# First feed-forward product of the last 1024 tokens as seven half-size products, with PSUM tiles and SBUF taken over from attention

## The chip, the cores and the metric

The kernel runs on one core of one Trainium2 chip. The metric is the device time of one execution in microseconds (us). The engines are called by their short names: PE (TensorE; its weight loads are listed apart as PEld), DVE (VectorE), ACT (ScalarE), POOL (GpSimd) and SP (the queue that issues most transfers). PSUM is the memory that PE writes its sums to, SBUF the memory that all engines work in.

## What is computed

Attention for 8 batches of 8 heads, 576 tokens each, head size 64, with a threshold, and then a feed-forward layer over all 4608 tokens. All of it is fp32.

```python
scores = scale * np.matmul(q, k.transpose(0, 1, 3, 2))
thresh = np.max(scores, axis=-1, keepdims=True) - tau
scores = np.where(scores >= thresh, scores, -1000000000.0)
...
x = np.ascontiguousarray(attn_out.transpose(0, 2, 1, 3)).reshape(B * S, H * D)
h = x @ w_in                                # (4608, 512) @ (512, 2048)
g = h * (1.0 / (1.0 + np.exp(-1.702 * h)))
return (g @ w_out)                          # (4608, 2048) @ (2048, 512)
```

## The kernel before

**Attention** goes by pairs of heads, `n` from 0 to 31, four pairs to a batch. For a pair, PE makes scores by tiles of 128 keys and a last one of 64 (L376, L383), ACT copies them out of PSUM (`keep`, L406), DVE takes their greatest value in several steps (`in_groups` L420, `over_tiles` L426 and L431, `over_groups` L438 and L439), subtracts it (`sub`, L490 and L495), ACT masks and takes exponentials (L501, L505), PE multiplies by the values (`values`, L519), and DVE makes the sums of the exponentials (again L420 to L439), turns and inverts them (`one_group` L558, `spread_sums` L567 and L569) and writes the scaled result to the tiles `xT` (`place_x`, L586).

**The feed-forward layer** goes by blocks of 256 tokens, 0 to 17. For blocks 2 to 17, `feed_forward` first makes the hidden values: eight panels `j`, each of two times 128 of the 2048 hidden columns. A panel is eight matmuls of 128x128 by 128x256 (`mm1`, L601, each of them two PE instructions), one tanh on ACT (L610) and one combination on DVE (L613). The second product is then done in the Winograd form of Strassen's method: seven products of half size instead of eight (`product`, L691). The sums of its left operands are made on POOL (`s_sums` L669 to L671, `s_last` L676), the seven products are joined by DVE (`read`, L713; the first by ACT, L706), and two stores follow.

**The order of work** is written out by a planner. Each step is a `task` with an engine, a cost, a rank and the tasks that it follows; `run_in_order` plays them through with these costs and issues the instructions in the order that comes out. Each engine then executes its own list strictly in this order, and waits on semaphores. Feed-forward matmuls have the last rank on PE, so they fill what attention leaves, and four blocks are left when attention ends. The first tokens of block 14 are done when batch 6 is, those of blocks 15 to 17 when pair 31, the last, is placed.

**PSUM** is eight banks: `psA` has three tiles of two banks (scores, products with values), `psM` two tiles of one bank (all of the feed-forward layer). **SBUF** for attention comes from a pool `work`: score tiles `s_m` and `s_t`, raw and turned q and k, `mb`, `mbt`, `rc` and `v_m`.

Of the kernel before, what the change touches and what calls it, by code (L numbers as in the profile page):

```python
# [30 lines left out]
def kernel(  # L31
# [75 lines left out]
        for x in range(2)  # L107
# [16 lines left out]

    tasks = []
    NXT = 5
    limits = {"psA": 3, "psM": 2, "s_m": 8, "s_t": 2, "io": 2, "osb": 2, "xT": NXT, "mb": 1,
              "raw0": 1, "raw1": 1, "qkT0": 1, "qkT1": 1, "v_m": 2, "w64": 2, "mbt": 1, "row": 1, "kd": 1, "rc": 1, "v_t0": 1, "v_t1": 1}
    for x in ("raw0", "raw1", "qkT0", "qkT1", "mb"):
        limits[x + "_apart"] = 1  # L130
# [94 lines left out]
    offset = {"raw0": 0, "raw1": S, "qkT0": 2 * S, "qkT1": 3 * S, "mb": 4 * S}  # L225
    offset.update({f"s_m{t}": (6 + 2 * t) * S for t in range(NKT)})

    def home(n, tag, size, name, bufs, key=None):
        if n in APART:
            o = offset[key or tag]  # L230
            return spare[:, o : o + size]
        return work.tile([P, size], FP32, name=name, tag=tag, bufs=bufs)

    def own(n, *pools):
        return tuple(x + "_apart" for x in pools) if n in APART else pools
# [3 lines left out]

    def load_qk(n, which, queue):  # L240
        b, hp = divmod(n, NPAIR)
        name, src = (("q", q), ("k", k))[which]
        t = home(n, f"raw{which}", S, f"{name}_raw", 1)
        blocks = t.rearrange("p (c d) -> p c d", d=32)
        for h in range(2):
            for j in range(2):
                queue.dma_start(  # L247
                    out=blocks[ds(64 * h + 32 * j, 32), :, :],
                    in_=src[b, 2 * hp + h, :, ts(j, 32)].rearrange("(c p) d -> p c d", p=32),
                )  # L250
        raws[n, which] = t

    def load_v(n):
        b, hp = divmod(n, NPAIR)
        t = work.tile([P, NKT, 2, D], FP32, name="v_m", tag="v_m", bufs=2)
        for h in range(2):
            nc.sync.dma_start(
                out=t[:, :, h, :],
                in_=v[b, 2 * hp + h, 0:MAIN, :].rearrange("(c p) d -> p c d", p=P),
            )  # L260
            nc.sync.dma_start(
                out=v_t[n % 2][ts(h, D), h, :], in_=v[b, 2 * hp + h, MAIN:S, :]
            )
        vs[n] = t
# [90 lines left out]

    def prep(n, which):

        dst = home(n, f"qkT{which}", S, "qkT", 1)
        nc.vector.transpose(out=dst, in_=raws.pop((n, which)))  # L359
        mats[n, which] = dst  # L360

# [31 lines left out]

    def keep(n, t, c):
        if t == NKT:
            st = work.tile([P, S], FP32, name="s_t", tag="s_t", bufs=2)
            o = halves(st)
        else:
            if c == 0:
                st = home(n, "s_m", 2 * S, "s_m", 8, f"s_m{t}")  # L400
                st = st.rearrange("p (h s) -> p h s", h=2)
            else:
                st = sT[n, t]
            o = st[:, :, ts(c, SH)]
        sT[n, t] = st
        nc.scalar.copy(out=o, in_=pss.pop((n, t, c))[:, :, 0:SH])  # L406
# [15 lines left out]
    def over_tiles(n, op):  # L422

        pm, pt = stats[n, op]
        r = work.tile([P, 2 * QB], FP32, name="red", tag="red", bufs=2)
        nc.vector.tensor_reduce(  # L426
            out=r, in_=pm.rearrange("p t c -> p c t"), axis=AXL.X, op=op
        )
        for h in range(2):
            part = r[ts(h, D), ts(h, QB)]  # L430
            nc.vector.tensor_tensor(out=part, in0=part, in1=pt[ts(h, D), :], op=op)  # L431
        stats[n, op] = r

    def over_groups(n, op):
        r = stats[n, op]
# [24 lines left out]
        nc.vector.transpose(out=o, in_=f)  # L460

    def spread_max(n):
        mb = home(n, "mb", 2 * S, "mb", 1)
        nc.vector.transpose(
            out=mb, in_=stats[n, ALU.max].unsqueeze(2).to_broadcast([P, 2 * QB, 32])
        )
        mbs[n] = mb.rearrange("p (h s) -> p h s", h=2)
# [7 lines left out]
        )  # L475

    def row_in(n):
        mb = home(n, "mb", 2 * S, "mb", 1)
        mbt = work.tile([P, S], FP32, name="mbt", tag="mbt", bufs=1)
        row = rows.pop(n)  # L480
        nc.sync.dma_start(out=mb, in_=row.to_broadcast([P, 2 * S]))
        for h in range(2):
            nc.sync.dma_start(out=mbt[ts(h, D)], in_=row[:, ts(h, S)].to_broadcast([D, S]))
        mbs[n] = mb.rearrange("p (h s) -> p h s", h=2)
        mbts[n] = mbt
# [38 lines left out]
    def values(n, tiles):  # L524
        if 0 in tiles:
            pvs[n] = psA.tile([P, 2, 512], FP32, name="pv", tag="ps")
        v_m, pv = vs[n], pvs[n]
        by_values(
            n, lambda t, h: v_m[:, t, h, :], lambda h: v_t[n % 2][:, h, :],
            [pv[:, c, :] for c in range(2)], tiles,  # L530
        )

    def sums_by_pe(n, tiles, apart):
        if 0 not in tiles:
            ps = pss[n]
        elif apart:
            ps = [psM.tile([P, BANK], FP32, name="den", tag="mo") for _ in range(2)]
        else:
            d = psA.tile([P, 2, 512], FP32, name="den", tag="ps")
            ps = [d[:, c, :] for c in range(2)]  # L540
        pss[n] = ps
        by_values(n, lambda t, h: ones, lambda h: ones_t[:, h, :], ps, tiles)

    def one_row(n):

# [18 lines left out]
    def spread_sums(n):  # L564

        r = rcs[n]
        nc.vector.reciprocal(out=r, in_=r)  # L567
        rc = work.tile([P, S], FP32, name="rc", tag="rc", bufs=1)
        nc.vector.transpose(out=rc, in_=r.unsqueeze(2).to_broadcast([P, QB, 32]))  # L569
        rcs[n] = rc  # L570

# [77 lines left out]
            op0=ALU.add, op1=ALU.mult,  # L649
        )  # L650

    qa = [[g[:, f, :, ts(h, HT)] for f in range(2)] for h in range(2)]
    qb = [[w_out[:, ts(f, HF), ts(m, HM)] for m in range(2)] for f in range(2)]
    s1, s2 = sg
    s3, s4 = qa[1][0], s2
    t1, t2, t4 = tw
    t3 = qb[0][1]

# [6 lines left out]

    def s_sums(k):

        a11, a21, a22, u1, u2 = (y[:, ts(k, 2), :] for y in (qa[0][0], qa[1][0], qa[1][1], s1, s2))
        nc.gpsimd.tensor_tensor(out=u1, in0=a21, in1=a22, op=ALU.add)  # L669
        nc.gpsimd.tensor_tensor(out=u2, in0=u1, in1=a11, op=ALU.subtract)  # L670
        nc.gpsimd.tensor_tensor(out=a21, in0=a11, in1=a21, op=ALU.subtract)  # L671

    def s_last(k):

        a12, u = (y[:, ts(k, 4), :] for y in (qa[0][1], s2))
        nc.gpsimd.tensor_tensor(out=u, in0=a12, in1=u, op=ALU.subtract)  # L676


    P1, P2, P6, P7, P4, P5, P3 = range(7)
    PRODUCTS = [  # L680
        (qa[0][0], qb[0][0], 0, 0), (qa[0][1], qb[1][0], 1, 0), (s2, t2, 0, 1), (s3, t3, 1, 1),
        (qa[1][1], t4, 0, 0), (s1, t1, 1, 0), (s4, qb[1][1], 0, 1),
    ]
    banks = {}

    def product(x, js):
        left, right, k, o = PRODUCTS[x]
        if x == k and js[0] == 0:
            banks[k] = psM.tile([P, BANK], FP32, name="ops", tag="mo")
        for j in range(*js):  # L690
            nc.tensor.matmul(  # L691
                banks[k][:, ts(o, HM)], lhsT=left[:, j, :], rhs=right[:, j, :],
                start=(j == 0), stop=(j == HF - 1),
            )

    def read(x):


        if x == P1:
# [1 line left out]
                osbs[i] = work.tile([P, d_model], FP32, name="osb", tag=f"osb{i}", bufs=1)  # L701
        (c11, c12), (c21, c22) = ([osbs[i][:, ts(m, HM)] for m in range(2)] for i in range(2))
        k, h = PRODUCTS[x][2:]
        ps = banks[k][:, ts(h, HM)]
        if x == P1:
            nc.scalar.activation(out=c21, in_=ps, func=AF.Copy, scale=0.5)  # L706
            return
# [116 lines left out]
    def feed_forward(blk):  # L824
# [3 lines left out]
        for j in range(HF):  # L828
# [11 lines left out]
            )  # L840
            if j % 2:
                sums.append(task("POOL", 2.5, FIRST, s_sums, j // 2, after=[gelus[j - 1], gelus[j]]))
        reads = [None] * 7

        order = [(P1, 0), (P1, 2), (P1, 3)]
        order += [(x, p) for x in range(P2, 7) for p in range(2)]
        for x, p in order:
            js = ((0, 4), (4, 8), (4, 7), (7, 8))[p]
            after = ffn[-1:] + t_ready
            if x in (P1, P2, P4):  # L850
                after += [gelus[j] for j in range(*js)]
            elif x == P3:
                after.append(lasts[p])
            else:
                after += sums[2 * p : 2 * p + 2]

            after += [reads[y] for y in range(x) if PRODUCTS[y][2:] == PRODUCTS[x][2:]]
            ffn.append(task(
                "PE", FFU / 4 * (js[1] - js[0]), LAST, product, x, js, after=after,
                take=("psM",) if x in (P1, P2) and p == 0 else (),  # L860
            ))
            last_mm2[p % 2] = ffn[-1]
            if p in (0, 2):
                continue
            if x == P6:
                lasts = [task("POOL", 1.6, FIRST, s_last, k, after=ffn[-1:]) for k in range(2)]
            if x == P1:
                a = task("ACT", 0.35, FIRST, read, x, after=ffn[-1:], take=("osb", "osb"))
            else:
                a = task(  # L870
                    "DVE", 0.84 if x == P5 else 0.42, FIRST, read, x, after=ffn[-1:] + reads,
                    give=("psM",) if x >= P5 else (),
                )
            reads[x] = a
        for i, x in ((1, P5), (0, P3)):
            task("SP", 0.6, FIRST, store, blk, i, after=[reads[x]], give=("osb",), lag=2.2)

    gelus = {}
    next_blk = 0
# [3 lines left out]
    for n in range(NP):  # L883
# [107 lines left out]
            "DVE", 1.1, r, place_x, n, after=[a, pv], take=("xT",) * len(new), give=("psA", "rc")  # L991
        )
        while hp == NPAIR - 1 and (next_blk + 1) * BLK <= (b + 1) * S:
            if next_blk >= PLAIN:
                feed_forward(next_blk)
            elif next_blk == PLAIN - 1:
                first_blocks()
            next_blk += 1
# [31 lines left out]
```

## Time and profile before

| what | us |
|---|---|
| median of 4 runs (1391.75 to 1392.04) | 1391.87 |
| the profiled execution | 1391.97 |
| its span, from the first instruction to the last | 1390.0 |
| PE busy in the span | 1344.5 |
| DVE busy | 1053.9 |
| ACT busy | 634.2 |
| POOL busy | 295.8 |

The span is shorter than the execution by 1.97 us, which lie before the first and after the last instruction. The profile lists instructions by engine and by the line of the kernel that issued them. Its views used here are the groups by line (count, busy time, mean duration in ns, and the idle time of the engine ahead of them), the chain of waits that ended last (in order of time), the timeline (start, duration, engine, line, and in brackets the idle time just before and what ended it) and busy time by windows with the clock that was granted to PE (1.00 is full). A matmul's end is modelled, and consecutive matmuls overlap: what one adds is read from the distance of the starts.

### The profile page before, as it was taken

The page shows a single profiled execution, that of the slowest core. Times are in us where ns is not written, and L with a number is a line of the kernel's source. Part 1 is how long each engine was busy: PE and PEld are TensorE (multiplying, and loading weights), DVE is VectorE, ACT ScalarE, POOL GpSimd, SP SyncE. Part 2 cuts the span into 40 slices and gives each one's busy share as a digit, 9 for nine tenths or more (in the row PEclk, how much of TensorE's full clock was granted, in tenths as well). Part 3 has the DMA queues.
Part 4 walks back from the last instruction along what each step waited for, and adds up shares of the span by engine and source line. Part 5 has one row for each costly group of instructions (what it writes and reads, how often), then busy time and mean ns, then how long its engine had stood idle before and what let it go on. Part 6 is the DMA issues. An engine that isn't in the chain of part 4 may idle for free.

```text
span 1390.0 us, 18051 instructions
## 1 busy us (share of the span) xinstructions
PE 1344.5 (97%) x6856; PEld 1016.3 (73%) x6856; DVE 1053.9 (76%) x1776; ACT 634.2 (46%) x806; POOL 295.8 (21%) x374
## 2 busy tenths in 40 slices
PE   5778999899999999999999999999999999999999
PEld 3446764477777777777777777777777778888887
DVE  7989999978888888889888888888888887111111
ACT  5964663555454545454545455444545453100100
POOL 1122212212121213122212122131213121211211
PEclk9889999999999999999999999999999999999999
DMA  8784972211111111111111011111110100000000
GB/s 174 201 241 134 304 239 67 68 23 20 41 27 41 27 41 25 35 26 34 29 35 29 18 42 26 42 26 42 26 42 18 42 0 16 1 16 16 1 16 16
DMA packets 205377, 78.70 MB, mean 57 GB/s; under 512 B 192747, under 2 KB 192747, under 8 KB 205291
## 3 DMA queue, kind: packets, MB, share of 16 engines
q1 hardware_dynamic: 195723, 43.71, 15.0%
q0 software_dynamic: 7200, 33.55, 7.1%
q8 instruction: 54, 0.88, 0.3%
q10 hardware_dynamic: 2368, 0.30, 0.2%
q14 instruction: 32, 0.26, 0.1%
HBM read 68.05 MB, written 9.47 MB: 56 GB/s over the span
## 4 chain that ended last, share of the span: by engine, by line
PE 85%; DVE 10%; DMA 2%; issue 1%; SPq 1%; ACT 0%; POOL 0%; ACTq 0%; DVEq 0%; POOLq 0%
PE hps L601 32%; PE ops L691 28%; PE pv L519 9%; PE ps L383 9%; PE hps L641 4%; DVE part L420 2%; PE ps L376 2%; DVE s_m L490 1%; DMA k_raw<-in_k_dram 1%; DMA arena<-in_moe_w_out_dram 1%; SPq L247 1%; DVE arena L340 1%; DVE red L439 1%; DVE w_in L348 0%; PE den L519 0%
## 5 line engine op out<-in xcount | busy, mean ns | idle before, releaser
L601 PE MATMUL hps<-xT,w_in 128*128 128x256 f32 x2048 | 457.5, 381 | 0.0
L601 PEld LDWEIGHTS hps<-xT,w_in 128*128 128x128 f32 x2048 | 385.2, 190 | 69.5 <-issue 18.5
L420 DVE TRANSPOSE_TENSOR_REDUCE part<-s_m 128x36 f32<-128x1152 f32 x228 | 304.7, 1355 | 71.2 <-ACT s_m L406 70.5
L406 ACT COPY s_m<-ps 128x576 f32<-128x576 f32 x240 | 141.2, 641 | 264.0 <-PE ps L383 262.6
L691 PE MATMUL ops<-w_out,arena 128*128 128x256 f32 x1024 | 234.1, 382 | 0.0
L610 ACT ACTIVATE th<-hps 128x512 f32<-128x512 f32 x144 | 85.5, 593 | 292.4 <-PE hps L601 271.6
L691 PEld LDWEIGHTS ops<-w_out,arena 128*128 128x128 f32 x1024 | 192.3, 190 | 36.1 <-issue 10.4
L669 POOL TENSOR_TENSOR arena<-arena 128x256 f32<-128x256 f32 x64 | 51.9, 811 | 611.0 <-DVE arena L613 611.0
L490 DVE TENSOR_TENSOR s_m<-s_m,mb 128x1152 f32<-128x1152 f32 x120 | 180.4, 1540 | 0.8
L691 PE MATMUL ops<-arena 128*128 128x256 f32 x768 | 171.0, 379 | 0.0
L383 PE MATMUL ps<-qkT 64*128 64x288 f32 x960 | 150.6, 435 | 18.1 <-DVE qkT L359 8.4
L501 ACT ACTIVATE s_m<-s_m 128x1152 f32<-128x1152 f32 x120 | 137.3, 1156 | 66.3 <-DVE s_m L490 66.2
L613 DVE SCALAR_TENSOR_TENSOR arena<-th,hps 128x512 f32<-128x512 f32 x128 | 85.8, 670 | 100.9 <-ACT th L610 100.9
L691 PEld LDWEIGHTS ops<-arena 128*128 128x128 f32 x768 | 145.9, 190 | 19.8
L505 ACT ACTIVATE s_m<-s_m,shift,scl 128x1152 f32<-128x1152 f32 x120 | 158.4, 1339 | 1.4
L383 PEld LDWEIGHTS ps<-qkT 64*128 64x128 f32 x960 | 83.8, 189 | 76.5 <-issue 46.4
L519 PE MATMUL pv<-s_m,v_m 128*64 128x288 f32 x960 | 126.0, 414 | 2.1 <-issue 2.1
L713 DVE SCALAR_TENSOR_TENSOR osb<-ops,osb 128x256 f32<-128x256 f32 x112 | 44.5, 408 | 86.0 <-PE ops L691 85.7
L519 PEld LDWEIGHTS pv<-s_m,v_m 128*64 128x64 f32 x960 | 67.1, 138 | 56.3 <-issue 14.8
L676 POOL TENSOR_TENSOR arena<-arena 128x512 f32<-128x512 f32 x32 | 62.6, 1963 | 111.3 <-PE ops L691 111.2
L623 PE MATMUL ops<-w_out,arena 128*128 128x512 f32 x128 | 60.0, 621 | 2.4 <-DVE w_out L348 2.4
L671 POOL TENSOR_TENSOR arena<-arena 128x256 f32<-128x256 f32 x64 | 60.0, 937 | 0.0
(97 smaller groups left out, 1072.9 us busy)
## 6 DMA issues: line engine op xcount, KB each, us to landing
out_dram<-osb SPq DMA_DIRECT2D x36, 256.0 KB, 2.0
q_raw<-in_q_dram SPq DMA_DIRECT2D x120, 72.0 KB, 2.3
k_raw<-in_k_dram SPq DMA_DIRECT2D x116, 72.0 KB, 2.3
v_m<-in_v_dram SPq DMA_DIRECT2D x64, 128.0 KB, 2.4
w_out<-in_moe_w_in_dram POOLq DMA_DIRECT2D x12, 512.0 KB, 5.6
arena<-in_moe_w_out_dram POOLq DMA_DIRECT2D x12, 512.0 KB, 6.1
w_out<-in_moe_w_in_dram POOLq DMA_DIRECT2D x12, 511.6 KB, 7.3
arena<-in_moe_w_out_dram POOLq DMA_DIRECT2D x12, 511.6 KB, 6.9
```

The costliest lines, as they stand in the source:

```text
L383: nc.tensor.matmul(ps[:, h, 0:SH], lhsT=kT[ts(h, D), ts(t, P)], rhs=qT[ts(h, D), ts(c, SH)], start=True, stop=True,)
L406: nc.scalar.copy(out=o, in_=pss.pop((n, t, c))[:, :, 0:SH])
L420: nc.vector.tensor_reduce(out=o, in_=i, axis=AXL.X, op=op, apply_transpose=True)
L490: nc.vector.tensor_tensor(out=s, in0=s, in1=mb, op=ALU.subtract)
L501: nc.scalar.activation(out=s, in_=s, func=AF.Prelu, alpha=STEEP)
L505: nc.scalar.activation(out=s, in_=s, func=AF.Exp, scale=scl, bias=shift)
L519: nc.tensor.matmul(o[c][ts(h, D), 0:SH], lhsT=lhsT, rhs=rhs, start=(t == 0), stop=(t == NKT),)
L601: nc.tensor.matmul(hidden[j][:, ts(f, BLK)], lhsT=w_in[:, c, ds((f * HF + j) * P, P)], rhs=xTs[blk][:, c, :], start=(c == 0), stop=(c == N ...
L610: nc.scalar.activation(out=ths[j], in_=hidden[j], func=AF.Tanh, scale=GELU_SCALE / 2)
L613: nc.vector.scalar_tensor_tensor(out=g[:, :, j, :], in0=two(ths.pop(j)), scalar=1.0, in1=two(hidden.pop(j)), op0=ALU.add, op1=ALU.mult,)
L676: nc.gpsimd.tensor_tensor(out=u, in0=a12, in1=u, op=ALU.subtract)
L691: nc.tensor.matmul(banks[k][:, ts(o, HM)], lhsT=left[:, j, :], rhs=right[:, j, :], start=(j == 0), stop=(j == HF - 1),)
```

## The change

Blocks 14 to 17 no longer go through `feed_forward` one by one, but through `two_blocks` by twos. The first product of 512 tokens is then a product of a 2x2 matrix of quarters (hidden halves by input halves) with another (input halves by blocks), and it is done by seven half-size products too. For each panel these are seven products of two matmuls (`product1`), in place of sixteen matmuls. Each product has a PSUM tile of its own, taken in turn from `psA` and `psM`, five in all. ACT copies the first product to SBUF, DVE adds the other six on (seven additions a panel, `read1`), and tanh and `gelu1` now read from SBUF, once for each of the two blocks. The sums of quarters of `w_in` are made once (four of 128x512 on DVE for the first two panels, twelve on POOL for the rest), those of `xT` four times 128x512 on DVE for each two blocks. The second block's hidden values are held in SBUF, and its sums for the second product (`s_sum1`) are done on DVE. The new SBUF tiles lie in `arena2`, which replaces the pool's attention tiles: these become fixed places in it, with the same number of buffers, handed on in order. The second product is as before, in `psM` for the first of two blocks, in `psA` for the second.

```diff
+    room, end = {}, 0
+    for tag, size, bufs in (
+        ("s_m", 2 * S, 8), ("s_t", S, 2), ("raw0", S, 1), ("raw1", S, 1), ("qkT0", S, 1),
+        ("qkT1", S, 1), ("mb", 2 * S, 1), ("mbt", S, 1), ("rc", S, 1), ("v_m", NKT * 2 * D, 2),
+    ):
+        room[tag] = [(end + x * size, size) for x in range(bufs)]
+        end += bufs * size
+    arena2 = const.tile([P, end], FP32, name="arena2")
...
+    W_SUMS = [
+        (wc[0], wq[1][0], wq[1][1], ALU.add), (wc[1], wc[0], wq[0][0], ALU.subtract),
+        (wc[2], wq[0][0], wq[1][0], ALU.subtract), (wc[3], wq[0][1], wc[1], ALU.subtract),
+    ]
+    def w_sum(x, k, engine):
+        o, a, b = (y[:, :, ts(k, 2 * P)] for y in W_SUMS[x][:3])
+        engine.tensor_tensor(out=o, in0=a, in1=b, op=W_SUMS[x][3])
...
+    def x_sum(blk, x):
+        b11, b12, b21, b22 = (x_quarter(blk, d, h) for d in range(2) for h in range(2))
+        u1, u2, u4 = xsum
+        o, a, b = ((u1, b12, b11), (u2, b22, u1), (b12, b22, b12), (u4, b21, u2))[x]
+        nc.vector.tensor_tensor(out=o, in0=a, in1=b, op=ALU.subtract)
+    BANK_OF = ("psA", "psM", "psA", "psM", "psA")
+    def product1(blk, j, x):
+        b11, b12, b21, b22 = (x_quarter(blk, d, h) for d in range(2) for h in range(2))
+        left, right = (
+            (wq[0][0], b11), (wq[0][1], b21), (wc[1], xsum[1]), (wc[2], b12),
+            (wq[1][1], xsum[2]), (wc[0], xsum[0]), (wc[3], b22),
+        )[x]
...
+        for c in range(2):
+            nc.tensor.matmul(
+                places[j, x], lhsT=left[:, c, ts(j, P)], rhs=right[:, c, :],
+                start=(c == 0), stop=(c == 1),
+            )
+    def read1(j, x):
...
+        for o, a in sums[x]:
+            nc.vector.tensor_tensor(out=o, in0=ps, in1=a, op=ALU.add)
...
+    def s_sum1(x):
+        (a11, _), (a21, a22) = qas[1]
+        o, a, b = ((s1, a21, a22), (s2, s1, a11), (a21, a11, a21))[x]
+        nc.vector.tensor_tensor(out=o, in0=a, in1=b, op=ALU.subtract if x else ALU.add)
...
+    def two_blocks(blk):
+        b = -(-(blk + 1) * BLK // S) - 1
+        xs = [placed[n] for n in range(NP)]
+        first, xd = not done_w, []
+        for x in range(4):
+            if first:
+                done_w.append([task("DVE", 0.66, LAST - 1.0, w_sum, x, 0, nc.vector, after=done_w[-1:][0] if done_w else xs)])
+            after = (xd[-1:] or xs) + (done_w[x][:1] if first else []) + last_product1
+            xd.append(task("DVE", 0.66, LAST - 1.0, x_sum, blk, x, after=after))
+        if first:
+            for k in range(1, HF // 2):
+                for x in range(4):
+                    after = xs + done_w[x - 1][-1:] + done_w[x][-1:]
+                    done_w[x].append(
+                        task("POOL", 1.5, FIRST, w_sum, x, k, nc.gpsimd, after=after)
+                    )
...
         while hp == NPAIR - 1 and (next_blk + 1) * BLK <= (b + 1) * S:
-            if next_blk >= PLAIN:
+            if next_blk >= TAIL:
+                if (next_blk - TAIL) % 2:
+                    two_blocks(next_blk - 1)
+            elif next_blk >= PLAIN:
                 feed_forward(next_blk)
```

## The prediction

> **What bounds the kernel now.** I read the page first, then the chain of waits from 1150 us on, then the timeline there. The page has PE busy for 97% of the span:
>
> ```profile
> PE 1344.5 (97%) x6856; PEld 1016.3 (73%) x6856; DVE 1053.9 (76%) x1776; ACT 634.2 (46%) x806; POOL 295.8 (21%) x374
> ```
>
> The chain of waits over the end of the run (start, duration, engine, tile, line, count) is PE alone, without a gap, up to the last read:
>
> ```profile
> 1175.76 3.65 PE ops L691 x16
> 1179.41 27.63 PE hps L601 x128
> 1207.03 24.17 PE ops L691 x112
> ...
> 1334.81 27.63 PE hps L601 x128
> 1362.43 24.19 PE ops L691 x112
> ```
>
> So blocks 14 to 17 lie behind attention (the last product with values ends at 1175.8) and are bound by PE: 27.63/128 = 0.216 us an instruction. What PE saves there is saved in full, and what makes PE wait there is paid in full. DVE is busy for 8 of each 50 us then, and has room.
>
> **What it removes.** The built program has 3396 matmuls for 3428, 32 fewer, two instructions each: 64 x 0.216 = **13.8 us** less on PE, in four blocks. Up to PE's 2949th matmul (the end of block 13) all five engines' lists stand in the same order as before, with the same waits, but for some loads that wait for one matmul less. The new places of attention's tiles therefore cost nothing, and block 14, which began at 1179.4 after pair 31 was placed (L586, ended 1176.8), loses no early start.
>
> **Panels in their steady state.** A panel is 28 instructions, 28 x 0.216 = 6.05 us of PE. Its DVE work is seven additions at 0.42 (L713 and L586 take 0.42 for 128x256 out of PSUM) and two `gelu1` at 0.69 (L613): 4.3 us. ACT has a copy at 0.38 (L706) and two tanh at 0.60: 1.6 us. The longest loop: the last product of a panel ends, its read 0.42, first `gelu1` 0.69, second tanh done by then or 0.1 later, second `gelu1` 0.69, and only then the next panel's reads, 1.9 us on, when its second product (at 1.73) has just ended. A PSUM tile comes round after five products, 3.5 us after its product ended; the latest read takes 0.6 of that. PE waits for none of it, with 2 us to spare. A wait before every two matmuls: the nearest row is the third product of before (L691, second to fourth piece), which waits for POOL every two matmuls and still has 3.62 us for 16 instructions like the rest, so I take 0. The other end is the row of scores (L383), with 18.1 us idle before 240 groups, 0.075 each; 112 products would lose 8.4 us. The second block's three sums of 128x1024 on DVE (about 1.25 us from L490's 1.35 for 1152) have 3.5 us and more until PE wants them, as one product of the second round takes 16 x 0.216 = 3.46 us: 0.
>
> **The start of the first two blocks.** Here PE must wait, since nothing is left to fill it. Products 1 and 2 need no sums: 1.73 us, till 1181.0. Product 3 needs two sums of weights and two of tokens. All four stand on DVE's list behind pair 31's placing and behind the last read of block 13, which ends at 1179.87:
>
> ```profile
> 1172.96 0.19 DVE L439 TENSOR_TENSOR red<-red,fold 64x36 f32<-64x36 f32 x1
> ...
> 1173.61 0.71 DVE L558 TENSOR_SCALAR r<-red 32x18 f32<-32x18 f32 x4
> ...
> 1175.81 0.95 DVE L586 TENSOR_TENSOR xT<-pv,rc 128x64 f32<-128x64 f32 x4 [0.37 <-PE pv L519]
> 1179.45 0.42 DVE L713 SCALAR_TENSOR_TENSOR osb<-ops,osb 128x256 f32<-128x256 f32 x1 [2.69 <-PE ops L691]
> ```
>
> A sum of 128x512 from SBUF is bounded by L490 (1.35 for 1152 with POOL at rest) and L492 (0.757 for 576), which differ by 1.03 ns an element: 0.69, of which 0.08 overlap the next; I take 0.65. Between them stands the read of product 2 (0.42). If nothing else happens, product 3 begins at 1179.9 + 4 x 0.65 + the wait for product 2 (0.5) + 0.42 = 1183.5, 2.5 to 3.0 us late; product 4 waits 0.4 more for its pair of sums, product 5 1.4 more for one sum, one read, one sum. That is 4.5 us.
>
> **But POOL is in the way.** Its twelve sums of weights, 128x512 each, follow its last old instruction directly. Their real waits are short: the first two only for exponentials that ended by 1134, the others for products with values of pair 31, from 1171.9 on, since their places are pair 31's score tiles. So two run from 1163.5, and ten from 1171.9 to about 1185 without a pause (1.27 us each, L676 in the quiet end). What POOL then does to DVE this trace shows, at 268 us (four POOL sums of 128x1024 in a row; start, duration):
>
> ```profile
> 268.05 0.18 DVE L438 COPY fold<-red 64x36 f32<-64x36 f32 x1
> 268.26 2.24 DVE L439 TENSOR_TENSOR red<-red,fold 64x36 f32<-64x36 f32 x1
> 270.53 2.27 DVE L438 COPY fold<-red 32x36 f32<-32x36 f32 x1
> 272.83 2.28 DVE L439 TENSOR_TENSOR red<-red,fold 32x36 f32<-32x36 f32 x1
> 275.14 2.79 DVE L558 TENSOR_SCALAR r<-red 32x18 f32<-32x18 f32 x4
> ```
>
> ```profile
> 268.06 4.71 POOL L664 TENSOR_TENSOR arena<-w_out,arena 128x1024 f32<-128x1024 f32 x2
> 272.72 4.64 POOL L664 TENSOR_TENSOR w_out<-w_out 128x1024 f32<-128x1024 f32 x2
> ```
>
> Each of DVE's small steps (0.17 to 0.19 alone) lasts until the POOL instruction in flight has ended, and POOL's next one slips in before DVE's next. L420, L569 and L586 are not held. Pair 31 has just this chain: two L431, two each of L438 and L439, four L558, ten steps that took 2.0 us from 1172.36. The first two POOL sums hold L495 at 1164.1, so it starts some 0.5 late, at 1172.9. One step waits for the third sum; two more slip through while the fourth waits for its values (1173.6); seven are left, each behind one sum: from 1175.0 seven ends at 1.25 apart, the last at 1182.5. Then L567 to L586, 2.4 us as before: placed at 1184.9. Read 0.42, first sum, read of product 2, three more sums, less overlaps: 1188.3. Product 3 starts near 1188.4 instead of 1181.1: **7.3 us** idle, then 0.4 and 1.4 as above, and 0.1 at 1167 where a product of block 13 waits for the delayed reads: **9.2 us**. If only one of the four L558 is held, it is 3.75 us less; if every step is held in full and adds its own 0.17, 1 us more.
>
> **The clock after the gap.** A PE gap costs more than itself (idle time before in brackets):
>
> ```profile
> 213.85 5.97 PE L623 MATMUL ops<-w_out,arena 128*128 128x512 f32 x10 [2.38 <-DVE w_out L348]
> ...
> 231.25 20.76 PE L623 MATMUL ops<-w_out,arena 128*128 128x512 f32 x48
> ...
> 280.25 2.29 PE L383 MATMUL ps<-qkT 64*128 64x288 f32 x8 [6.37 <-DVE xT L586]
> 282.47 3.22 PE L623 MATMUL ops<-w_out,arena 128*128 128x512 f32 x4
> ```
>
> By windows of 1 us the granted clock is 0.50 from 214 to 216 and from 279 to 285. Ten L623 took 5.97 where 48 took 20.76 (4.3 for ten): 1.6 us lost after 2.38 idle. After 6.37 idle, 1.05 + 1.23 = 2.3. Products 3 and 4 run within DVE's chain, so part is hidden; I take **1.8** (0 to 2.3).
>
> [...]
>
> **Sum.** -13.8 + 9.2 + 1.8 = -2.8. From the profiled execution's own 1391.97 (its span of 1390.0 and 1.97 around it; 0.10 over the median): **1389.2 us**.
>
> **Rivals.** (1) POOL's sums hold little: the L558 go together, or DVE wins the place between. For it: L490 in company with L676 lost only 0.2. Against: the four rows at 268 us. Then -13.8 + 4.5 + 0.4 for a held step or two + 1.6 clock = -7.3: 1384.7. (2) DVE becomes the bound of the panels, so that it is slower than before. Place: the chain of nine DVE instructions a panel, 4.3 of 6.05 us. It decides from 0.19 us more on each; at 0.25 more, with semaphores between, a panel takes 6.55 and 16 panels lose 8.0: 1397.2. For it: seven of them depend on each other and on PE; against: 1.75 us of room, and L713's 0.42 is with a wait. (3) The start is costlier (every step held, the clock low for longer): 2 to 4 us more, 1391 to 1393.
>
> **How the numbers follow.** A measurement of this kernel can tell about 0.2%, 2.8 us, from no change, that is 1389.1 on the fast side, where my forecast lies. Forecast 0.62 (1387 to 1391; faster 0.28, same 0.34), rival 1 0.18 (faster), rival 2 0.13 (slower), rival 3 0.07 (same 0.06, slower 0.01). Faster 0.46, same 0.40, slower 0.14. The range for 8 in 10 takes in rival 1 and rival 3 and leaves out rival 2: 1384.4 to 1393.0.
>
> **What would show it.** Right: an idle PE of 6 to 8 us before the third product of the first panel, released by DVE; L558 of pair 31 four times as long or more; twelve sums on POOL from 1163 to 1185; clock 0.50 for 3 to 7 us; then no PE idle time over 0.1 us to the end, and 48.4 us for each eight panels. Wrong: PE idle inside panels, waiting for `read1` (rival 2); pair 31 placed by 1178 (rival 1); a gap between the rounds of the second product.

## The result, and the profile after

| | us |
|---|---|
| before, median of 61 runs (1389.85 to 1395.14) | 1391.92 |
| after, median of 41 runs (1387.27 to 1391.97) | **1389.72** |
| after / before | 0.9983, 95% interval 0.9979 to 0.9988 |
| profiled execution of after, its span | 1389.5, 1387.7 |

The change makes the kernel 0.17% faster, 2.2 us; 1389.2 was forecast. Of the 13.8 us that the saved matmuls are worth, 11.8 are lost again in one place, the first panel of blocks 14 and 15. The page's first part for the changed kernel:

```profile
PE 1334.3 (96%) x6792; PEld 1005.7 (72%) x6792; DVE 1124.2 (81%) x1906; ACT 639.5 (46%) x822; POOL 298.7 (22%) x362
```

PE has 64 instructions fewer, but only 10.2 us less of busy time, although 64 x 0.216 is 13.8: what is left runs 3.6 us longer in all. The chain of waits from 1239 us on (start, duration, engine, tile, line, count) is PE alone again, without a hole:

```profile
1239.27 24.17 PE ops L825 x112
...
1335.97 24.17 PE ops L825 x112
```

The waits of PE from 1155 us to the end (total, times, longest) lie ahead of this: the first line is two waits in the first panel of blocks 14 and 15, the second a wait for a read of block 13, at 1166.8.

```profile
PE ps L743 <- DVE arena L726: 7.7, 2, 6.5
PE ops L825 <- DVE osb L847: 0.3, 1, 0.3
```

Between the two pairs of second products lie the eight panels of blocks 16 and 17, each for both blocks: 1287.62 to 1335.97, 48.35 us where before took 2 x 27.63 = 55.26. That is 6.9 us gained, half of the 13.8. The other half is not to be seen for blocks 14 and 15, whose panels start at 1179.00 and whose second products start at 1239.11 in the timeline (the chain counts both 0.16 later): 60.1 us. PE's timeline there (in brackets the idle time before, and what ended it):

```profile
1179.00 1.03 PE L743 MATMUL ps<-xT,w_in 128*128 128x256 f32 x4
...
1187.40 2.05 PE L743 MATMUL ps<-arena 128*128 128x256 f32 x4 [6.51 <-DVE arena L726]
1189.24 1.91 PE L743 MATMUL ops<-xT,arena 128*128 128x256 f32 x4
1192.36 2.04 PE L743 MATMUL ps<-arena,w_in 128*128 128x256 f32 x4 [1.21 <-DVE arena L726]
...
1196.81 1.03 PE L743 MATMUL ps<-xT,w_in 128*128 128x256 f32 x4
```

A product takes 0.86 from start to start at full clock. Product 3 starts 8.40 us after product 1 instead of 1.73, and four products are listed with some 2 us each instead of 1. The DVE timeline ahead of it:

```profile
1173.72 1.32 DVE L471 COPY fold<-red 32x36 f32<-32x36 f32 x1
...
1176.32 3.84 DVE L595 TENSOR_SCALAR r<-red 32x18 f32<-32x18 f32 x4
...
1181.38 0.95 DVE L623 TENSOR_TENSOR xT<-pv,arena 128x64 f32<-128x64 f32 x4
...
1183.54 1.45 DVE L726 TENSOR_TENSOR arena<-xT 128x512 f32<-128x512 f32 x1
1184.91 1.75 DVE L717 TENSOR_TENSOR arena<-arena,w_in 128x512 f32<-128x512 f32 x1
1186.58 0.68 DVE L726 TENSOR_TENSOR arena<-xT,arena 128x512 f32<-128x512 f32 x1
```

L595 is the old L558: 3.84 us for four steps that took 0.71. POOL works from 1171.72 on, with one pause of 0.68 us (ten sums of 128x512, L717; the last is shown):

```profile
1184.39 1.71 POOL L717 TENSOR_TENSOR arena<-w_in,arena 128x512 f32<-128x512 f32 x1
```

POOL's last sum ends at 1186.1, and the DVE steps that follow are short again: L726 and L717 take 1.45 and 1.75 beside POOL's last two sums and 0.68 right after. And the clock, by windows (busy time of PE, PEld, DVE, ACT, POOL, then the granted clock):

```profile
1178.00:1185.00 7.00, 2.89 (x14) 2.20 (x12) 6.81 (x13) 0.37 (x1) 6.92 (x6) 1.00 0.11 40
...
1186.00:1195.00 9.00, 6.39 (x14) 4.71 (x15) 4.93 (x9) 0.09 (x1) 0.10 (x1) 0.50 0.01 2
```

PE is at full clock till 1185, at 0.86 for the next 1 us, at 0.50 to 1195 and at 0.52 for 1 us more, that is at half clock from 1185.7 to 1196.0: products 3 to 6 run in it. The loss is thus 60.1 - 48.3 = 11.8 us (48.3 is what the panels of these two blocks take without any wait, measured below).

### The profile page after: what moved, and what is told of

Its sections match the earlier page's. It is cut to its first block, busy times and chain, and to the rows that moved or that the text cites. A ratio compares the mean times of both kernels' runs of the same rounds, so it can differ in the third digit from the quotient of the medians.

```text
span 1387.7 us, 18139 instructions
## 1 busy us (share of the span) xinstructions
PE 1334.3 (96%) x6792; PEld 1005.7 (72%) x6792; DVE 1124.2 (81%) x1906; ACT 639.5 (46%) x822; POOL 298.7 (22%) x362
## 4 chain that ended last, share of the span: by engine, by line
PE 84%; DVE 10%; DMA 3%; SPq 1%; issue 1%; ACT 1%; DVEq 0%
PE hps L638 25%; PE ops L825 24%; PE pv L552 9%; PE ps L414 9%; PE ps L743 4%; PE hps L678 4%; PE ps L825 3%; PE ops L743 3%; PE ps L407 2%; DVE part L451 2%; DMA arena<-in_q_dram 2%; SPq L278 1%; DVE arena L523 1%; PE den L552 1%; DVE w_in L379 1%
## 5 line engine op out<-in xcount | busy, mean ns | idle before, releaser
L451 DVE TRANSPOSE_TENSOR_REDUCE part<-arena 128x36 f32<-128x1152 f32 x236 | 315.2, 1354 | 71.8 <-ACT arena L437 71.1
L638 PE MATMUL hps<-xT,w_in 128*128 128x256 f32 x1536 | 346.3, 382 | 0.0
L638 PEld LDWEIGHTS hps<-xT,w_in 128*128 128x128 f32 x1536 | 287.9, 190 | 56.3 <-issue 18.5
L437 ACT COPY arena<-ps 128x576 f32<-128x576 f32 x288 | 171.0, 641 | 292.2 <-PE ps L414 271.2
L534 ACT ACTIVATE arena<-arena 128x1152 f32<-128x1152 f32 (+1 forms) x160 | 168.2, 1060 | 74.9 <-DVE arena L523 68.9
L538 ACT ACTIVATE arena<-arena,shift,scl 128x1152 f32<-128x1152 f32 (+1 forms) x160 | 194.3, 1243 | 1.9
L523 DVE TENSOR_TENSOR arena<-arena 128x1152 f32<-128x1152 f32 x128 | 190.6, 1528 | 1.2 <-DMA arena<-row 0.5
L414 PE MATMUL ps<-arena 64*128 64x288 f32 x1024 | 162.3, 440 | 23.1 <-DVE arena L390 11.7
L791 POOL TENSOR_TENSOR arena<-arena 128x256 f32<-128x256 f32 x56 | 46.5, 830 | 570.3 <-DVE arena L650 468.7
L414 PEld LDWEIGHTS ps<-arena 64*128 64x128 f32 x1024 | 91.0, 192 | 86.6 <-issue 52.4
L552 PE MATMUL pv<-arena 128*64 128x288 f32 x960 | 125.5, 413 | 2.2 <-issue 2.2
L552 PEld LDWEIGHTS pv<-arena 128*64 128x64 f32 x960 | 66.8, 138 | 55.8 <-issue 13.8
L390 DVE STREAM_TRANSPOSE arena<-arena 128x576 f32<-128x576 f32 x64 | 48.3, 763 | 37.7 <-PE ps L407 35.3
L847 DVE SCALAR_TENSOR_TENSOR osb<-ops,osb 128x256 f32<-128x256 f32 x98 | 38.7, 406 | 34.9 <-PE ops L825 32.9
```

The source lines that it names most:

```text
L414: nc.tensor.matmul(ps[:, h, 0:SH], lhsT=kT[ts(h, D), ts(t, P)], rhs=qT[ts(h, D), ts(c, SH)], start=True, stop=True,)
L451: nc.vector.tensor_reduce(out=o, in_=i, axis=AXL.X, op=op, apply_transpose=True)
L523: nc.vector.tensor_tensor(out=s, in0=s, in1=mb, op=ALU.subtract)
L534: nc.scalar.activation(out=s, in_=s, func=AF.Prelu, alpha=STEEP)
L538: nc.scalar.activation(out=s, in_=s, func=AF.Exp, scale=scl, bias=shift)
L552: nc.tensor.matmul(o[c][ts(h, D), 0:SH], lhsT=lhsT, rhs=rhs, start=(t == 0), stop=(t == NKT),)
```

## The experiments

The theory: POOL's sums hold pair 31's small DVE steps and the first sums on DVE (a step is held when it lasts longer than alone beside a POOL instruction: in the changed kernel the small ones end within 0.05 us of POOL's end, L726 and L717 of the start 0.56 us behind it); the order on DVE makes the rest of the gap; the gap costs clock beside itself; the panels themselves are PE's. The rivals: POOL is incidental; the clock is not what makes the products slow; DVE's many new reads are what takes the gain. All ratios are to the kernel before, which took 1391.83 beside the first four kernels, 1391.79 beside the next four and 1391.71 beside the last two.

**POOL held back.** A one-column copy on POOL waits for the last sum of tokens, and the twelve sums of weights come after it.

```diff
+    def hold_pool():
+        nc.gpsimd.tensor_copy(out=held_by, in_=xsum[2][:, 0, 0:1])
...
+            held_task = task("POOL", 0.3, FIRST, hold_pool, after=xd[-1:])
-                    after = xs + done_w[x - 1][-1:] + done_w[x][-1:]
+                    after = xs + done_w[x - 1][-1:] + done_w[x][-1:] + [held_task]
```

> The twelve sums of weights on POOL are made to wait for the last of DVE's start sums, by a small POOL copy that reads it. Theory (POOL's sums hold pair 31's last steps on DVE, then PE idles and its clock falls): pair 31 is placed at 1176.8 again, product 3 of the first panel waits 2.5 to 3.0 us instead of 6.5, the start loses 4.5 us plus up to 1.6 for the clock instead of 11.8, so 5.5 to 7.3 us less than the changed kernel: 1382.4 to 1384.3. Rival (the gap is DVE's own start: eight sums and the reads behind the last read of block 13, and POOL is only beside it): within 1 us of the changed kernel, 1388.7 to 1390.7.

Measured: 1385.38 (1382.84 to 1385.53, 5 runs), 0.9948 [0.9935, 0.996]; the profiled execution 1382.84. The four L595 take 0.71 again, and pair 31 is placed at 1176.8. DVE's timeline, then PE's:

```profile
1173.69 0.71 DVE L595 TENSOR_SCALAR r<-red 32x18 f32<-32x18 f32 x4
...
1179.53 0.43 DVE L847 SCALAR_TENSOR_TENSOR osb<-ops,osb 128x256 f32<-128x256 f32 x1 [2.69 <-PE ops L825]
...
1181.68 0.42 DVE L759 TENSOR_TENSOR arena<-ops,arena 128x256 f32<-128x256 f32 x1 [1.13 <-PE ops L743]
```

```profile
1184.05 1.10 PE L743 MATMUL ps<-arena 128*128 128x256 f32 x4 [2.83 <-DVE arena L726]
...
1187.50 1.10 PE L743 MATMUL ps<-arena,w_in 128*128 128x256 f32 x4 [1.21 <-DVE arena L726]
```

POOL's part is shown: without its company no step is long. What is left is order: DVE sits idle for 2.69 us, since block 13's last read (L847) stands ahead of the sums, and then for 1.13 us, since the read of product 2 stands between them. The median lies above the range expected; the profiled execution, the lowest of the five, lies inside it. Two more executions, below, show part of the reason.

**Order as well.** POOL stays held. Block 13's last read goes behind the second sum of tokens, and so behind four of the eight sums, and the panel's first reads behind the last sum of tokens.

```diff
+            tasks[last_read[0]][5].append(xd[1])
-                        after=ffn[-1:] + reads, give=bank,
+                        after=ffn[-1:] + reads + (xd[-1:] if first and j == 0 else []), give=bank,
```

> As e1_hold, and DVE makes its eight start sums right behind pair 31's placing, four of them ahead of the last read of block 13, the other four ahead of the first panel's reads. Theory: placed at 1176.8, the four sums for product 3 done by 1179.3, before it is due at 1181.0, all eight by 1182.4, no PE gap, no low clock, 13.8 us less than before but for a few tenths: 1377.8 to 1379.2. Rival of e1_hold (DVE's own start): the same gap as there, or at best half of it: 1383 or more. Rival (DVE falls behind in the first panels, as the reads start late): 1380 to 1383.

Measured: **1377.68** (1377.34 to 1380.07, 4 runs), 0.9903 [0.9889, 0.9916]: the fastest kernel of the study, 12.0 us under the changed one. PE's timeline from 1178 has no idle time left:

```profile
1180.44 1.03 PE L743 MATMUL ps<-arena 128*128 128x256 f32 x4
...
1182.17 1.03 PE L743 MATMUL ps<-arena,w_in 128*128 128x256 f32 x4
```

The panels of blocks 14 and 15 start at 1178.72 and their second products at 1227.06: 48.3 us. So the whole 13.8 us were there to be had.

**Order alone,** with POOL where the change put it (the diff is the last one, on the changed kernel).

> The fourth kernel of the two edits: the changed kernel with block 13's last read put behind two of the first panel's sums and the panel's first reads behind the last of these sums, as in the version that took 1377.7, but with POOL's twelve sums of weights where the change put them, beside pair 31's small steps. My theory (POOL's holding and the order on DVE add up, and POOL's part is the larger): pair 31 is placed at 1182.3 as in the changed kernel, product 3 starts 0.4 to 1 us earlier than there (1186.4 to 1187.0), product 5 follows without the 1.2 us of idle time, the clock falls after the gap: 1386.5 to 1388.7. Rival (the order on DVE is what counts, so that it brings most of the 12 us by itself): under 1383.

Measured: 1387.0 (1386.82 to 1388.86, 5 runs), 0.9967 [0.9954, 0.998]. Pair 31 is placed at 1183.6 here, not 1182.3 as in the changed kernel: all four L595 are held, not three.

```profile
1176.43 5.01 DVE L595 TENSOR_SCALAR r<-red 32x18 f32<-32x18 f32 x4
```

Product 3 therefore starts at 1187.6, later than expected, product 5 without idle time. The two edits bring 4.3 and 2.7 us alone by the medians, and 12.0 together: the sums of the start need both the place on DVE and DVE's own speed, and as long as either fails PE waits (2.83 and 1.21 us in the profiled execution with POOL held, 6.62 with the order alone), and the clock can fall (0.50 from 1185.4 to 1192.3 with the order alone).

**The gap filled.** Fourteen more matmuls (6.04 us, into a PSUM tile that nothing reads) after product 2 of the first panel. Nothing else differs from the changed kernel.

> Fourteen more matmuls (6.04 us) behind product 2 of the first panel, into a PSUM tile that nobody reads, so that PE is busy in the gap; all else as in the changed kernel. Theory (the 128x256 matmuls behind the gap take twice as long because the clock was halved): clock 1.00 behind the gap, the four slow products back to 0.86 us, 2.5 to 3.3 us less than the changed kernel, 1386.4 to 1387.2. Rival (they are slow because DVE and POOL work at the same time): unchanged, 1389.2 to 1390.2.

Measured: 1386.5 (1386.3 to 1387.69, 5 runs), 0.9965 [0.9951, 0.9978]: 6.04 us more work, and 3.2 us less time than the changed kernel. PE's timeline:

```profile
1180.93 6.21 PE L750 MATMUL ps<-xT,w_in 128*128 128x256 f32 x28
1187.61 1.10 PE L743 MATMUL ps<-arena 128*128 128x256 f32 x4 [0.47 <-DVE arena L726]
...
1191.06 1.10 PE L743 MATMUL ps<-arena,w_in 128*128 128x256 f32 x4 [1.21 <-DVE arena L726]
```

Product 3 starts 8.40 us after product 1, exactly as in the changed kernel, but at a clock of 1.00. From product 1 to the second products it is 56.8 us instead of 60.1: **the clock after the gap costs 3.3 us**, and the gaps in themselves 56.8 - 48.3 = 8.5.

**The last two blocks alone.** `TAIL = NBLK - 2`: blocks 14 and 15 stay as before, so the start has pair 31 long behind it.

> Only blocks 16 and 17 by seven products, blocks 14 and 15 as before, so that all sums can be made beside block 14's and 15's matmuls. Theory (the panels themselves run at PE's pace, and the start alone ate the gain): the full gain of one half, 6.9 us less than before: 1384.5 to 1385.5. Rival (PE loses time inside the panels or between the rounds): 1387 or more.

Measured: 1386.22 (1384.71 to 1386.9, 5 runs), 0.9958 [0.9945, 0.997]. The profiled execution has a span of 1382.9, 7.1 under before's 1390.0, near the 6.9 of two blocks, and no product of its panels waits. But this execution is the lowest of the five: by the medians the gain is 5.6 us. The median is 0.7 above the range expected; five runs spread over 2.2 us do not tell whether that is more than spread.

**POOL in the kernel before.** Ten sums of 128x512 on POOL, into a tile that is no longer read, released by pair 31's products with values.

```diff
+    def idle_sum(x):
+        nc.gpsimd.tensor_tensor(
+            out=sT[NP - 1, 0][:, :, 0:256], in0=w_in[:, 0:2, ts(x % 4, 256)], in1=w_in[:, 2:4, ts(x % 4, 256)], op=ALU.add
+        )
```

> The kernel before with ten POOL sums of 128x512 added (two operands in SBUF, as the changed kernel's sums of weights, written into a tile that is no longer read), from about 1172 us on, while pair 31's small DVE steps run; nothing waits for them and nothing else is changed. My theory (POOL's sums themselves hold those steps): the four L558 of pair 31 go from 0.71 us together to 3 us or more, its placing by L586 ends 4 to 6 us later than the 1176.7 of the kernel before, and the time stays within 1 us of before, since block 14's first product in that kernel does not read what is placed last before 1180. Rival (the memory's lay-out or the panels' own work on DVE made the steps long, not POOL): the four L558 stay at 0.7 us together and the placing at 1176.7.

Measured: 1392.54 (1390.92 to 1394.89, 10 runs), 1.0001 [0.9992, 1.0011]. Five of the ten sums fell on the chain, from 1174.39 to 1181.27. POOL's and DVE's timelines:

```profile
1174.39 6.88 POOL L879 TENSOR_TENSOR s_m<-w_in 128x512 f32<-128x512 f32 x5 [8.02 <-PE pv L519]
```

```profile
1175.25 0.66 DVE L431 TENSOR_TENSOR red<-red,part_t 64x18 f32<-64x18 f32 x2
1175.95 1.17 DVE L438 COPY fold<-red 64x36 f32<-64x36 f32 x1
1177.16 0.19 DVE L439 TENSOR_TENSOR red<-red,fold 64x36 f32<-64x36 f32 x1
...
1178.79 2.70 DVE L558 TENSOR_SCALAR r<-red 32x18 f32<-32x18 f32 x4
...
1182.71 0.95 DVE L586 TENSOR_TENSOR xT<-pv,rc 128x64 f32<-128x64 f32 x4
```

From the first L431 to pair 31's placing (the end of L586) it is 8.4 us instead of 4.4. That is 4.0 us, the low end of the 4 to 6 expected, and L558 has 2.70, not 3. POOL's sums alone, without the change, lengthen the same steps, and cost nothing there that ten runs can tell, because block 14's first product does not wait for them. The hold is POOL's; that it costs time is the change's.

**DVE's room in the panels.** Every `gelu1` twice, and three times (same operands, same output).

```diff
-        nc.vector.scalar_tensor_tensor(
-            out=gs[h][:, :, j, :], in0=two(ths.pop((j, h))), scalar=1.0,
-            in1=hs[j % 2][:, :, h, :], op0=ALU.add, op1=ALU.mult,
-        )
+        th = two(ths.pop((j, h)))
+        for _ in range(2):
+            nc.vector.scalar_tensor_tensor(
+                out=gs[h][:, :, j, :], in0=th, scalar=1.0,
+                in1=hs[j % 2][:, :, h, :], op0=ALU.add, op1=ALU.mult,
+            )
```

> The changed kernel with every gelu1 of the last four blocks done twice (same inputs, same output): 32 more DVE instructions of 0.69 us, 1.4 us more on DVE in each of the 16 panels, 4.25 + 1.4 = 5.65 us against PE's 6.05. My theory (DVE has 1.8 us of room a panel, so it decides only from there on): 0 to 0.5 us more than the changed kernel's 1389.7 for the 16 panels together, 1389.5 to 1391. Rival (what counts is the chain of read, gelu1 and next reads, which leaves no more than the room that the plan shows between a product's end and its read, so DVE decides already here): PE waits inside panels, 0.5 us or more in each, 1397 or more.

> The changed kernel with every gelu1 of the last four blocks done three times: 2.8 us more on DVE a panel, 4.25 + 2.8 = 7.05 us against PE's 6.05. My theory: DVE is now the bound of the panels, 1.0 us each, 16 panels: 16 us more than the changed kernel, 1404 to 1408, with PE idle inside the panels waiting for read1. Rival (DVE has more room than the sum of its instructions says, for instance because these overlap): under 1397.

Measured: twice 1389.98 (1387.44 to 1392.36, 10 runs), 0.9987 [0.9977, 0.9996], the changed kernel's time; three times 1405.88 (1403.73 to 1407.1, 4 runs), 1.0098 [1.0083, 1.0113], 16.2 us more. With `gelu1` twice, PE has only the waits of the changed kernel. With it three times, PE waits in the panels for `read1`, L759 (waits of PE: total, times, longest):

```profile
PE ps L743 <- DVE arena L759: 7.5, 8, 1.4
PE ops L743 <- DVE arena L759: 3.7, 4, 1.4
```

So 1.4 us more DVE a panel is free and 2.8 is not; the point from which DVE decides lies between, as the sum of instructions (4.25 against 6.05) had it. DVE's reads are not where the gain went.

**Two more executions of the kernel with POOL held,** unchanged, since its five times were 1382.84, 1383.22, 1385.38, 1385.51 and 1385.53.

> The version with POOL held, once more, for its trace: its five times lay in two groups, 1382.8 to 1383.2 and 1385.4 to 1385.5, and the trace at hand is of the first, where the clock stayed at 1.00 behind gaps of 2.8 and 1.2 us. My theory (the same gaps lower the clock in some executions, as the 2.4 us gap did in the kernel before): a span near 1381 with the clock at 1.00 from 1180 to 1200 us, or one near 1383.6 with a stretch at 0.50 there. Rival (the groups come from elsewhere, such as the waits for loads before 300 us): a span near 1383.6 with the clock at 1.00 there, and product 1 of block 14 later by some 2.4 us.

> The same kernel a third time, with the same two readings: a span near 1383.6 either goes with a stretch of the clock at 0.50 between 1180 and 1200 us (my theory) or with a later product 1 of block 14 at a clock of 1.00 (rival).

Measured: 1384.85 (span 1383.0) and 1383.97 (span 1382.2). Busy time by windows, the clock third from the right. First the execution profiled above, then the first and the second of the two:

```profile
1184.00:1186.00 2.00, 1.94 (x8) 1.36 (x8) 1.92 (x4) 0.00 (x0) 0.00 (x0) 1.00 0.00 0
```

```profile
1184.00:1186.00 2.00, 1.15 (x3) 1.00 (x4) 1.91 (x4) 0.00 (x0) 0.00 (x0) 0.59 0.00 0
```

```profile
1184.00:1186.00 2.00, 1.40 (x4) 0.59 (x2) 1.18 (x4) 0.00 (x0) 0.00 (x0) 0.50 0.00 0
...
1188.00:1190.00 2.00, 2.00 (x6) 1.62 (x5) 0.42 (x1) 0.63 (x1) 1.99 (x2) 0.50 0.00 0
```

From 1184 on the first stays at 1.00; the second is at half clock for 3.4 us, till 1187.8; the third, from 1183.9, for 6.8 us, till 1190.7. The gaps are nearly the same in all three (2.83 and 1.21, 2.85 and 1.21, 2.85 and 1.21). From product 1 to the second products they take 53.1, 54.3 and 55.9 us: the clock costs nothing, 1.2 and 2.7. That is the theory, but not all of it: in the third execution the span is only 1.1 us longer than in the first, because block 14 began 1.6 us earlier, and in the second 0.8 of the 1.9 us lie ahead of block 14. So the start of block 14 varies too, and neither new execution has a span of 1383.6.

## Why the prediction was right

The time, 1389.2 against 1389.72, and the mechanism were right. That the time came so close is partly luck: the start was 0.7 us cheaper than forecast and the clock 1.5 us dearer, and these errors cancel in part, on an effect of only 2.2 us. The time alone would also have shown little, since the range for 8 in 10 holds even no change at all. What shows the mechanism are the traces and the experiments.

- **The panels, -13.8: right.** 48.35 instead of 55.26 us for eight panels of blocks 16 and 17, no wait in them, and 48.3 for those of blocks 14 and 15 once the start is repaired. Zero for the wait before every two matmuls was right; the other end, 8.4, is excluded.
- **The start, 9.2: 8.5 measured,** by the kernel with the gap filled: 6.7 us (8.40 - 1.73) before product 3 where 7.3 were forecast, and 1.8 after it, as forecast. Pair 31 was placed at 1182.3 and not 1184.9: of the seven steps that I had each behind a POOL sum, L471, L472 and three of four L595 were held. In return L726 and L717 were held too, for 0.8 and 1.1 us; I had let POOL end in time for them. These are two errors of opposite sign in the step "seven are left, each behind one sum" and what follows it, and that they nearly cancel is luck. The wait in block 13 was 0.34 us, not 0.1.
- **The split of the start** (4.5 from order, the rest from POOL): right. With POOL held 4.8 us remain at a clock of 1.00.
- **The clock, 1.8 (0 to 2.3): mis-sized,** 3.3 measured. The row at 280 us has PE busy soon after the gap. Here a second idle time of 1.21 us follows and the clock stays at 0.50 for 10.2 us, where I had 3 to 7. That the second idle time keeps it low is not shown, but fits: with the order alone, where it is missing, the clock is low for 6.8 us (1185.4 to 1192.3), and in the two kernels with `gelu1` repeated, where it is there, products 3 to 6 are slow again (listed with 1.83 to 2.05 us each) till 1196.1 and 1196.7; with `gelu1` three times the clock is 0.60 on average from 1184 to 1196, which is 9.6 us at 0.50. Against it, the kernel with POOL held has both idle times and 0, 3.4 and 6.8 us.
- **Sum:** -13.8 + 8.5 + 3.3 = -2.0, and block 14 began 0.2 us earlier: -2.2, against -2.3 between the two spans (1387.7 and 1390.0); -2.8 was forecast.
- **Rival 1** (POOL holds little) is excluded by the four L595, rival 2 (DVE bounds the panels) by `gelu1` done twice; its point of 1.75 us more DVE a panel agrees with 1.4 free and 2.8 not. Rival 3 (a costlier start, by 2 to 4 us) holds for the clock alone, and there by 1.5.
- **`gelu1` beside POOL:** the second L768 of a panel took 1.19 to 1.26 us beside POOL's L791 and 0.69 without. It is hidden: PE has no wait in those panels.

Shown by runs: POOL's hold, the order on DVE, the clock's price, DVE's room. Not shown: why in one execution three L595 are held and in another four, and how many of the runs of the changed kernel owe their 1387.3 to 1392.0 to the clock. Their granted clock, a mean over the whole execution, points that way: it is 0.985 to 0.988 in the runs up to 1388.1 us and 0.983 to 0.986 in the others. Where in the execution the difference lies, no trace of theirs shows.

## What to carry to other kernels

When a change puts new work at the seam where one stage ends and the next begins, look for what that work needs first and who is busy then: here 12 us hung on where two kinds of sums stood in the lists of two engines. Work that nobody needs soon, like POOL's weight sums, belongs behind the chain that is urgent, even if its engine is idle, when its instructions hold those of that chain, as POOL's sums do here (3.84 and 5.01 us for four L595 that take 0.71 without them). And a gap on PE is to be counted with the slow products that can follow it: 3.3 us on gaps of 8.5 here, some 40% more, and 0, 1.2 and 2.7 us in the three executions with POOL held.

## What the runs showed of the hardware

- A copy, a tensor_scalar and a tensor_tensor of 0.17 to 0.19 us on DVE each lasted until POOL's sum in flight ended (1.16 to 1.32 us for the copies and the tensor_tensor), and a chain of them went one per POOL instruction, though some slipped through: 3.84 and 5.01 us for the same four L595. POOL suffered too: a sum of 128x512 took 1.27 alone (L676 of the kernel before, at 1215.75) and 1.71 and 1.75 beside DVE's sums of the same size (L717 of the changed kernel, at 1184.39 and 1182.68).
- Nearly the same idle time of PE, 2.85 us in two executions and 2.83 in a third of one kernel, lowered the clock in the two and not in the third. The low stretches are 3.4, 6.8 and 10.2 us long (1184.4 to 1187.8, 1183.9 to 1190.7, 1185.7 to 1196.0). Why one execution kept its clock and the others did not, and what sets the length of a low stretch, no run shows.
- Extra matmuls (6.04 us) in a gap that PE must wait through anyway kept the clock at 1.00 and made the kernel 3.2 us faster.
